# A plain second chunk instead of Strassen's, later rounding of weights, and keys of four pieces transposed by TensorE

## Chip, cores, metric

One core of one Trainium2 chip. The metric is the device time of one execution in microseconds, of the slowest core (there is one). The span in a profile is from the first to the last instruction and some 1 to 2 us shorter than the time. Lower is better.

## The reference, cut to what matters

```python
# attention: batch 8, heads 8, 576 positions, head_dim 64
scores = q @ k.T / 8
ret    = (scores * gamma_h ** (i - j) for j <= i, else 0) @ v      # no softmax
x = ret.transpose(0, 2, 1, 3).reshape(4608, 512)
# feed-forward: d_model 512, d_ff 2048
h = x @ w_in
g = h * erf(softplus(h))
out = g @ w_out                                                    # all in float32
```

## The kernel before

Tokens come in nine chunks of 512, each of four *pieces* of 128 (`PC = 4`); pieces 0 to 3 are chunk 0. A piece passes three stages: `transposes` (q and k with head_dim on partitions), `scores` (TensorE; VectorE masks the result into `sT`), and `outputs` (TensorE; VectorE scales the result into the chunk's `x`). These stages are laid between the matrix products of the feed-forward part, which runs in four groups (`g`) of hidden columns over the nine chunks: `First` is x times w_in, `Second` is g times w_out. The code calls a group's blocks of w_in `wa` and those of w_out `wb`; g is formed as t x s, with t for h and s for erf(softplus(h)). The attention stages share four buffers in PSUM, the memory that TensorE's results go to here; VectorE or ScalarE has to read a buffer before it is written again. In the first group all of this overlaps; in the other three, x is read back from HBM.

Both products use a Strassen form: seven block products in place of eight, at the price of sums on VectorE. Chunk 0 of the first group alone is `plain`, because its sums of weights are not ready:

```python
def plain(self):                       # 4 d-blocks x 4 accumulators x 2 = 32 matmuls
    for dc in range(n_dc):
        slots = (A12, A22) if dc // 2 else (A11, S3)      # S3 holds A21 until the sums are made
        for n in range(4):
            ...                                           # 2 matmuls, then yield

def operands_x(g, c):                  # Strassen: four sums of x on VectorE (three if g > 0)
    tt(t1, b12, b11, ALU.subtract)
    tt(t2, b22, t1, ALU.subtract)
    tt(b12, b22, b12, ALU.subtract)
    tt(t4, b21, t2, ALU.subtract)

def sums_in(a11, s3, a12, a22, s1, s2, s4):               # four sums of w_in's blocks
    ...
    tt(s3, a11, s3, ALU.subtract)      # from here on A21 is gone
```

Weights are rounded before use, in steps: ScalarE two passes, VectorE four (lines L252 to L265), then a product and an addition that GpSimd does for w_out (`wb`) and for all later groups. Keys and queries of pieces 0 to 7 come as rows and are transposed by TensorE and copied by ScalarE; from piece 8 on they come as *squares* of 32x32 and are transposed by VectorE:

```python
SQUARES = 2 * PC
...
if i >= SQUARES:
    nc.vector.transpose(out=tT..., in_=squares[:, :, :, :SQ])
else:
    nc.tensor.transpose(pt[:, p, :], flat(t[name][:, 2 * p : 2 * p + 2, :]), ident)   # 4 of them
    nc.scalar.copy(out=tT, in_=pt)
```

The order of the beginning is a string (`a` one attention stage, `p` one step of the plain chunk, `w` one load of weights, a digit so many rounding steps). The order matters because VectorE's work stands in the traces in the order in which the program emits it: in the prediction's timeline a rounding of w_out, 57.01 to 61.03 us, comes before the masked scores of 61.95 us that TensorE waits for.

## Time and profile before

| | before |
|---|---|
| time, median of 4 runs | 1034.19 us (1033.63 to 1035.70) |
| TensorE busy | 1017.5 of a span of 1035.3 us |
| VectorE busy, whole span | 65% |
| VectorE busy, 67 to 97 us | 29.5 of 29.8 us |
| start of piece 7's scores; of the second block's T2 product | 57.46; 97.08 us |

How to read it: the share over the span says that TensorE is the bound and VectorE is not. The line for 67 to 97 us says the opposite for that stretch. The prediction below shows these lines. One more line marks the end of the stretch, the first product of g's sums with w_out (T2); columns of this timeline are start, duration, engine, line, operation, operands:

```profile
97.08 1.99 PE L594 MATMUL a<-wb,s 128*128 128x256 f32 x8
```

The order of TensorE's instructions is the same in both kernels up to piece 7's outputs and from T2 on, so I measure both kernels between the start of piece 7's scores and T2: 97.08 - 57.46 = 39.62 us before.

### The profile page before, as it was taken

Reading aid. Unit: us, or ns where it says so; the run is one execution under the profiler, and the core shown is the slowest. Engines: PE = TensorE matmul, PEld = TensorE weight load, DVE = VectorE, ACT = ScalarE, POOL = GpSimd, SP = SyncE. Lnnn points to the kernel's source line nnn. Section 1 sums busy time; section 2 is a strip of 40 time slices with the busy share of each in tenths; the row PEclk is TensorE's granted clock in tenths of the full one; section 3 lists DMA queues with packets and bytes.
Section 4 is the critical chain, followed back from the end, with each engine's and each line's share of the span. In section 5 each row is a group of like instructions: output and inputs, shape, how many; then the busy total and the mean of one; then the engine's idle time right before and its main releaser. Section 6 shows DMA issues by size and latency. Waiting matters only on the chain.

```text
span 1035.3 us, 15922 instructions
## 1 busy us (share of the span) xinstructions
PE 1017.5 (98%) x6322; PEld 875.1 (85%) x6322; DVE 677.5 (65%) x1063; ACT 388.1 (37%) x477; POOL 124.3 (12%) x122
## 2 busy tenths in 40 slices
PE   8988999999999999999999999999999999999998
PEld 7767888887788888888888888888888888888887
DVE  3898778777777555667666656666666655555555
ACT  2353133242343544433434334444443333333332
POOL 2142112222312110100001000100100000000000
PEclk9989999999999999999999999999999999999999
DMA  9989979979983544444445444444433334444433
GB/s 192 202 200 223 248 150 251 216 179 245 216 211 124 204 142 142 143 142 144 169 161 161 155 147 142 145 159 167 143 122 122 123 122 131 132 130 133 127 88 117
DMA packets 148778, 167.27 MB, mean 162 GB/s; under 512 B 97632, under 2 KB 123360, under 8 KB 140640
## 3 DMA queue, kind: packets, MB, share of 16 engines
q1 hardware_dynamic: 147696, 165.47, 57.2%
q8 instruction: 50, 0.82, 0.4%
q10 hardware_dynamic: 1008, 0.79, 0.3%
q14 instruction: 24, 0.20, 0.1%
HBM read 119.02 MB, written 47.19 MB: 161 GB/s over the span
## 4 chain that ended last, share of the span: by engine, by line
PE 85%; DMA 7%; DVE 3%; SPq 3%; issue 1%; ACT 1%; POOL 0%; DVEq 0%; POOLq 0%
PE a L594 23%; PE a L486 22%; PE g L594 11%; PE g L486 11%; PE e L594 6%; PE e L486 5%; DMA raw_v<-in_v_dram 3%; PE s L339 2%; PE o L357 2%; DMA raw_qs<-in_q_dram 1%; DMA raw_ks<-in_k_dram 1%; SPq L130 1%; SPq L144 1%; PE o L380 1%; PE o L368 1%
## 5 line engine op out<-in xcount | busy, mean ns | idle before, releaser
L486 PE MATMUL a<-x,wa 128*128 128x256 f32 x1120 | 266.4, 381 | 0.0
L486 PEld LDWEIGHTS a<-x,wa 128*128 128x128 f32 x1120 | 211.8, 190 | 29.6
L594 PE MATMUL a<-wb,s 128*128 128x256 f32 x864 | 205.7, 381 | 0.0
L594 PEld LDWEIGHTS a<-wb,s 128*128 128x128 f32 x864 | 162.9, 190 | 23.6 <-ACT o L608 0.7
L99 DVE TENSOR_TENSOR t<-g,t 128x512 f32<-128x512 f32 x70 | 48.2, 689 | 150.9 <-ACT t L516 113.1
L486 PE MATMUL g<-x,wa 128*128 128x256 f32 x560 | 133.1, 380 | 0.0
L486 PEld LDWEIGHTS g<-x,wa 128*128 128x128 f32 x560 | 105.7, 190 | 14.9
L99 DVE TENSOR_TENSOR o<-a,o 128x512 f32<-128x512 f32 x108 | 74.1, 686 | 50.5 <-PE a L594 50.5
L511 ACT COPY t<-a 128x512 f32<-128x512 f32 x35 | 20.5, 586 | 189.6 <-PE a L486 189.6
L99 DVE TENSOR_TENSOR t<-t,s 128x1024 f32<-128x1024 f32 x72 | 88.8, 1274 | 0.0
L555 ACT ACTIVATE s<-t 128x1024 f32<-128x1024 f32 x72 | 72.1, 1049 | 32.0 <-DVE t L99 32.0
L267 POOL TENSOR_TENSOR wraw<-wraw 128x512 f32<-128x512 f32 x28 | 29.7, 1059 | 433.8 <-DVE wraw L265 176.6
L99 DVE TENSOR_TENSOR x<-x 128x512 f32<-128x512 f32 x116 | 77.8, 703 | 1.2
L522 ACT COPY t<-a 128x512 f32<-128x512 f32 x35 | 20.5, 586 | 151.9 <-PE a L486 151.9
L559 ACT ACTIVATE s<-s 128x1024 f32<-128x1024 f32 x72 | 72.1, 1048 | 0.4
L594 PE MATMUL a<-wb,t 128*128 128x256 f32 x288 | 68.6, 381 | 1.1 <-DVE t L99 1.1
L594 PE MATMUL e<-wb,t 128*128 128x256 f32 x288 | 68.6, 381 | 0.0
L594 PE MATMUL g<-wb,s 128*128 128x256 f32 x288 | 68.6, 381 | 0.0
L594 PE MATMUL g<-wb,t 128*128 128x256 f32 x288 | 68.2, 380 | 0.0
L486 PE MATMUL e<-x,wa 128*128 128x256 f32 x280 | 66.8, 381 | 0.0
L99 DVE TENSOR_TENSOR o<-g,o 128x512 f32<-128x512 f32 x72 | 49.3, 684 | 25.7 <-ACT o L608 20.9
L99 DVE TENSOR_TENSOR sT<-s,cst 128x512 f32<-128x512 f32 x72 | 46.1, 680 | 29.7 <-PE s L339 29.7
(75 smaller groups left out, 1202.6 us busy)
## 6 DMA issues: line engine op xcount, KB each, us to landing
od<-o SPq DMA_DIRECT2D x54, 512.0 KB, 3.4
x<-xd SPq DMA_DIRECT2D x27, 1024.0 KB, 4.8
o<-od SPq DMA_DIRECT2D x27, 1024.0 KB, 5.1
raw_qs<-in_q_dram SPq DMA_DIRECT2D x96, 112.0 KB, 4.6
raw_ks<-in_k_dram SPq DMA_DIRECT2D x96, 112.0 KB, 4.3
xd<-x SPq DMA_DIRECT2D x9, 1024.0 KB, 5.4
raw_k<-in_k_dram SPq DMA_DIRECT2D x64, 128.0 KB, 4.5
raw_v<-in_v_dram SPq DMA_DIRECT2D x64, 128.0 KB, 4.5
```

The lines of the kernel that those rows point to most:

```text
L99: nc.vector.tensor_tensor(out=out, in0=in0, in1=in1, op=op)
L130: nc.sync.dma_start(out=t[part * SQ : (part + 1) * SQ, :, at : at + m - SQ], in_=tokens[:, :, d0 : d0 + m - SQ])
L144: nc.sync.dma_start(out=t[r0 : r0 + n, e::2, :], in_=heads.rearrange("h p d -> p h d"))
L267: engine.tensor_tensor(out=r_f, in0=high_f, in1=r_f, op=ALU.mult)
L339: nc.tensor.matmul(ps[e][:, p, :], lhsT=t["kT"][heads[e], p, :], rhs=t["qT"][heads[e], p, :], start=True, stop=True)
L357: nc.tensor.matmul(o[p % 2][heads[(e + p) % 2], p // 2, :], lhsT=t["v"][:, 2 * p + e, :], rhs=t["sT"][:, e, p, :], start=(p < 2), stop=(no ...
L486: nc.tensor.matmul(acc[:, j * TH : (j + 1) * TH], lhsT=weights["wa", self.g][:, a, d, j * P : (j + 1) * P], rhs=x[self.g, self.c][a][:, d, :],
L511: nc.scalar.copy(out=self.t1[:, 1], in_=self.a)
L522: nc.scalar.copy(out=self.t2[:, 0], in_=self.a)
L555: nc.scalar.activation(self.s[:, j], t, AF.Softplus)
L559: nc.scalar.activation(self.s[:, j], self.s[:, j], AF.Erf)
L594: nc.tensor.matmul(acc[:, tp, :], lhsT=left[:, j * TH + tp * P : j * TH + (tp + 1) * P], rhs=weights["wb", self.g][:, b, j, :], start=(sta ...
```

## The change

The intent: give the early stretch, where VectorE is the bound, less VectorE work and a better order. Three parts: the second chunk `plain` too, so that its sums of x and additions are not needed and the sums of wa can wait; rounding of w_out moved behind the attention stages that TensorE waits for; keys of pieces 8 to 11 (`SQUARES_K`) as rows through TensorE.

```diff
+    SQUARES_K = 3 * PC
...
                     t["qs"] = load_squares(i, "q", q)
-                    t["ks"] = load_squares(i, "k", k)
-                elif name == "v" or len(pieces[i]) == 1:
+                    if i >= SQUARES_K:
+                        t["ks"] = load_squares(i, "k", k)
+                elif name == "v" or i < SQUARES_K or len(pieces[i]) == 1:
...
-                yield src, "wa", g, a, dc % 2, sums_in if dc == n_dc - 1 else None
+                yield src, "wa", g, a, dc % 2, ["wa"] if g > 0 and dc == n_dc - 1 else []
...
-                    yield src, "wb", ..., sums_out if (f, j) == (1, GP - 1) else None
+                    sums = (["wb"] if g > 0 else ["wb", "wa"]) if (f, j) == (1, GP - 1) else []
...
+    PLAIN = 2                                   # operands_x: chunks 0 and 1 unsummed in HBM
-        if g == 0 or c == 0:
+        if g == 0 or c < PLAIN:
...
-    for what in "alkakakawkakakawaa3awwa2aaa5ppappawwppa5ppapp5awwcpp4a5ppapp5aa5s1":
+    for what in "alkakakawkakakawaa3awwa2aaa5ppappawwppa5ppapp5wawcppa5ppappaa5s":
...
     firsts[0].softplus()
+    firsts[0].erf()
     most[0] = before_chunk(3)
-    attend(after_chunk(1) + 1)
-    operands_x(0, 1)
-    for step, _ in enumerate(firsts[1].first()):
-        attend(done[0] + 1)
-        round_weights((4, 2)[step])
-    firsts[0].erf()
-    firsts[0].multiply()
+    attend(after_chunk(1))
+    store_x(1)
+    for step, _ in enumerate(firsts[1].plain()):
+        if step % 2 == 0:
+            attend(min(done[0] + 1, most[0]))
+        round_weights(int(step > 1))
+        if step == 4:
+            firsts[0].multiply()
+        elif step == 8:
+            firsts[0].sums()
     seconds[0].begin()
+    run(seconds[0].first(), (2, 2))
+    firsts[1].softplus()
+    most[0] = before_chunk(4)
-    for b, nxt in zip(blocks[1:], blocks[2:] + [None]):
+    for b, nxt in zip(blocks[2:], blocks[3:] + [None]):
```

More of the change, by code (lines that the diff above doesn't have):

```diff
@@ L198, in parts @@
                     src = [(slice(0, P), w_out[ft * P : (ft + 1) * P, :].rearrange("p (h o) -> p h o", h=2))]
-                    yield src, "wb", g, B21 if f else B11, j, sums_out if (f, j) == (1, GP - 1) else None
+                    sums = (["wb"] if g > 0 else ["wb", "wa"]) if (f, j) == (1, GP - 1) else []
+                    yield src, "wb", g, B21 if f else B11, j, sums
     def sums_in(a11, s3, a12, a22, s1, s2, s4):
@@ L271, in rounding @@
             yield
-            if sums:
-                for step, _ in enumerate(sums(*(w[:, i] for i in range(7)))):
+            for n in sums:
+                of = (sums_in if n == "wa" else sums_out)(*(operands(n, g)[:, i] for i in range(7)))
+                for step, _ in enumerate(of):
                     if step == 3:
-                        rounded.add((name, g))
+                        rounded.add((n, g))
                     yield
@@ L312, in transposes @@
             tT = t[name + "T"] = att.tile([P, NP, P], FP32, tag=name + "T", name=name + "T")
-            if i >= SQUARES:
+            if name + "s" in t:
                 for _, _, n, r0 in pieces[i]:
```

## The prediction

> **What bounds the kernel now.** I read the page's first part, then the table of stretches, then TensorE's waits, then the timelines of TensorE and VectorE where the waits are.
>
> First part of the page (engine, busy us, share of the span, instructions):
>
> ```profile
> PE 1017.5 (98%) x6322; PEld 875.1 (85%) x6322; DVE 677.5 (65%) x1063; ACT 388.1 (37%) x477; POOL 124.3 (12%) x122
> ```
>
> TensorE is busy for 1017.5 of 1035.3 us. All that a change can win without taking work from TensorE is the 18 us in which it stands still, and time in which it runs at a lower clock. The change adds work to TensorE, so the question is whether it removes more standing still than it adds.
>
> The table of stretches, core 0, columns PE, PEld, DVE, ACT, POOL busy, granted clock, DMA share, GB/s:
>
> ```profile
> 45.94:57.46 11.52, 11.52 (x110) 9.58 (x108) 10.99 (x19) 6.78 (x12) 2.56 (x3) 1.00 0.65 167
> 57.46:67.28 9.82, 5.72 (x68) 4.49 (x64) 7.77 (x13) 2.62 (x5) 6.10 (x6) 0.69 0.78 201
> 67.28:97.08 29.80, 26.70 (x251) 21.30 (x249) 29.52 (x47) 10.78 (x13) 10.03 (x8) 0.99 1.18 246
> 97.08:123.04 25.96, 25.96 (x252) 21.17 (x249) 19.72 (x31) 8.01 (x10) 6.29 (x7) 1.00 0.91 226
> ```
>
> Between 57 and 67 us TensorE is busy only 5.7 of 9.8 us and is granted 0.69 of its clock. From 67 to 97 us VectorE is busy 29.5 of 29.8 us: there VectorE is the bound, and nowhere else for so long. From 97 us on TensorE runs without a hole. Of the rest of the 18 us, about 2.5 us lie at 240, 275 and 281 us, 4.2 us after the last matmul, some 2.6 us in the first 26 us; the change touches none of these.
>
> TensorE's waits from 45 to 97 us (line, waited for, us, times, longest):
>
> ```profile
> PE o L357 <- POOL wraw L267: 4.1, 1, 4.1
> PE a L594 <- DVE t L99: 1.1, 1, 1.1
> PE o L357 <- issue: 1.1, 1, 1.1
> PE p L540 <- DVE wa L268: 0.7, 1, 0.7
> PE s L339 <- DVE kT L318: 0.6, 1, 0.6
> ```
>
> The longest is booked on GpSimd, but a wait for several semaphores goes to the one that came last by the profile. The timelines of TensorE and VectorE show the real one:
>
> ```profile
> 57.46 1.16 PE L339 MATMUL s<-qT,kT 64*128 64x128 f32 x16
> 62.72 2.52 PE L357 MATMUL o<-sT,raw_v 128*64 128x128 f32 x16 [4.09 <-POOL wraw L267]
> ...
> 57.01 1.15 DVE L256 TENSOR_SCALAR wb<-wb 128x512 uint32<-128x512 uint32 x1
> 58.19 1.65 DVE L260 SCALAR_TENSOR_TENSOR wb<-wraw,wb 128x512 uint32<-128x512 uint32 x1
> 59.88 1.15 DVE L265 TENSOR_SCALAR wraw<-wb 128x512 uint32<-128x512 uint32 x1
> ...
> 61.95 1.27 DVE L99 TENSOR_TENSOR sT<-s,cst 128x512 f32<-128x512 f32 x2
> ```
>
> Piece 7's scores are done at 58.6 us; the masked scores sT that its outputs need come only at 61.95 us, behind two rounds of rounding weights and the scaling of piece 6 in VectorE's order. VectorE is late because the program gave it four sums of wa (2.62 us from 50.66) and two roundings of wb before them.
>
> **What the Trainium skill says.** "TensorE: Matmul & The Clock Gate", Part 1: after about one idle window of 3.4 us the array falls to half its clock, and needs about as long a busy time to get it back. The trace agrees: after the 4.09 us hole the granted clock is 0.50 from 62.70 to 67.30 and 1.00 again from 69.7. "SBUF — State Buffer", Who interferes with whom: VectorE and GpSimd share a port pair as a lock, held for a whole instruction. The trace agrees: the L260 form takes 0.69 us alone and 1.65 beside GpSimd's product at 57.95. "VectorE: DVE Perf Modes", The three transpose paths: VectorE transposes in 32x32 blocks into SBUF, TensorE a full 128x128 into PSUM, so a copy must follow. Here VectorE's key transpose of a piece has a median of 1.09 us; four TensorE transposes start 0.44 us apart as a group (pt_q 46.91, pt_k 47.35, next 47.79) and ScalarE's copy takes 0.59 us.
>
> **The change, part by part.** The order of instructions shows that TensorE's sequence is the same up to the outputs of piece 7 and the same again from the second block's T2 product on (at 97.08 us before). So the gain or loss is made between 46 and 97 us.
>
> (a) Plain second chunk on TensorE. Strassen's seven products have 28 matmuls; the plain form has 32. Each is two instructions, and eight of them take 1.73 us when nothing else comes between (spacing in the chain, 330 us and later). Four matmuls more: +1.7 us, all on the path, since TensorE is full.
>
> (b) Keys by TensorE. Four pieces by 0.44 us: +1.8 us on TensorE. ScalarE gets four copies, 2.3 us, with 37% busy: hidden. VectorE loses 0.73 + 3 x 1.06 = 3.9 us.
>
> (c) VectorE loses besides: four sums of x (3.9 us at 69.48, 2.6 in other chunks) and three additions of t (2.0 us). With the keys, 9.8 us of the 46 us that it works from 50.7 to 97 us. In each later group one more sum of x, 0.7 us, in stages where VectorE is about 60% busy: nothing.
>
> (d) The four sums of wa move from 50.66 us to after the roundings; a rounding of wb moves behind each piece. So the masked scores of piece 6 come at about 50.8 and not 53.2, the first rounding of wb ends at about 54.3, and VectorE stands idle when piece 7's scores end at 58.6. The first sT then comes 0.65 us later: the 4.1 us wait becomes 0.7 to 1: -3.2 us. The clock is not lost: 4.6 us of work at 0.50 take 2.3, and the next 2.4 us at 0.87 save 0.3: -2.6 us.
>
> (e) The waits at 78.9, 83.1 and 86.1 us (0.65 + 1.13 + 1.05 = 2.8 us; the last is from a busy VectorE too) should mostly go, since the keys, the products t x s and the x sums no longer stand in a row there. I leave 0.8 us: -2.0 us.
>
> (f) DMA: the squares of keys of four pieces are not loaded (about 4 x 4 x 112 KB), piece 8's rows are (256 KB): 1.5 MB less at 246 GB/s, 6 us of a DMA that is saturated from 67 to 97 us. It pays for the earlier start of everything behind; I book no gain.
>
> Sum: +1.7 + 1.8 - 3.2 - 2.6 - 2.0 = -4.3 us. A second way: writing the new order down with the measured durations, from the end of piece 7's scores to the T2 product. Outputs of piece 7 end at about 62.1 (67.28 before); the stretch to T2 was 29.8 us, of which 2.8 waits and 0.5 lost clock, so 26.5 of work, plus 3.5 gives 30.0: T2 at about 92.1 against 97.08, -5.0 with no wait left, and -4.2 with 0.8. I take -4.5: **1029.5 us**.
>
> **Rivals.** First: new waits eat the gain. Three places: the second sum of wb needs GpSimd's last rounding, and VectorE stands behind it ahead of piece 10's sT; x of piece 8 goes into the buffer of chunk 0, whose store must have landed (by my account 69.5 to 71 us, wanted at 72.3); ScalarE has softplus and erf, 6.6 us with both table loads, in front of piece 8's key copy. Against it: each has 1 us or more of room in my account, and VectorE has 9 us less to do. If one or two fail, 2 to 4 us come back: 1032 to 1034. Second: the added TensorE work is all that is left, because the wait at 62.72 comes anyway, from raw_v or data. The raw_v that it also needs is ready at 60.7 us before, itself behind GpSimd's rounding; with the first rounding earlier this moves to about 58. If the hole stayed, the time would be 1034 + 3.5 - 2 = 1035.5. Third: DMA relief goes on and also removes the waits at 240 to 281 us, or VectorE's slack keeps all of (e): 1026 to 1027. Those late waits are for key squares of later pieces behind stores in one queue, whose order is unchanged, so I think this is less likely than the first.
>
> **Range and chances.** Best case, every hole from 57 to 97 us and half of the late ones gone: about 1025. Worst plausible, the rival with the hole left or a new one with its loss of clock: 1035. Eight in ten: 1025.0 to 1034.0. 2% is 20.7 us, more than all of TensorE's standing still, so faster by over 2% has a chance of 0.01; slower by as much would need several new holes with lost clock: 0.01; within 2%: 0.98.
>
> **What would show it.** Right: TensorE's instructions 24 more and busy time about the same or a little less (the slow instructions gone); no clock of 0.50 between 57 and 70 us; the outputs of piece 7 ending near 62 us and T2 near 92.5; VectorE's busy time some 8 us less; after T2 the same spacing as before. Step (d) is wrong if a hole over 3 us stays before the outputs of piece 7; (e) if TensorE waits over 1.5 us between there and T2; (f) if new waits for input pieces come after 100 us. A wait that lasts past one idle window anywhere in the stretch would cost its length and some 2.5 us of clock, and make the prediction wrong.

## The result, and the profile after

The changed kernel took 1028.08 us (1027.37 to 1028.72, 4 runs) against 1034.19: ratio 0.9938, 95% interval 0.9921 to 0.9956. Taken again (e12 below) it took 1027.16 against 1035.65, ratio 0.9918 (0.9904 to 0.9931). Ratios are the mean time of one kernel's runs over that of the other's of the same rounds, so not quite the ratio of the medians quoted. The results are correct. The intervals together show a gain of 0.4 to 1.0%.

First part of the page, after; then the table of stretches, with the same columns as before:

```profile
PE 1017.5 (99%) x6346; PEld 876.1 (85%) x6346; DVE 669.1 (65%) x1054; ACT 390.4 (38%) x481; POOL 123.7 (12%) x122
```

```profile
45.94:57.46 11.52, 11.52 (x119) 9.66 (x119) 7.95 (x15) 7.35 (x13) 4.29 (x4) 1.00 0.88 211
57.46:62.00 4.54, 3.57 (x60) 2.73 (x57) 4.03 (x9) 4.50 (x5) 1.25 (x3) 1.00 0.70 159
62.00:92.00 30.00, 29.88 (x278) 24.48 (x277) 24.11 (x43) 11.87 (x18) 11.48 (x12) 1.00 1.06 251
```

TensorE has 24 instructions more (8 matmul, 16 transpose) and the same busy time: the added work stands where matmuls at half clock stood. From 62 to 92 us it is busy 29.88 of 30 us at full clock, and VectorE is no longer full (24.1 of 30). TensorE's waits of the whole run:

```profile
PE idle L706 <- POOL ident masks.py:199: 1.4, 1, 1.4
PE o L361 <- POOL state L423: 0.8, 1, 0.8
PE pt_k L328 <- DMA raw_k<-in_k_dram: 0.7, 2, 0.4
PE p L546 <- DVE wa L271: 0.7, 1, 0.7
PE s L343 <- DVE kT L322: 0.2, 1, 0.2
```

The 4.1 us are 0.8, and the three waits of 0.6 to 1.1 us between piece 7's outputs and T2 have gone. TensorE's timeline at the same place as in the prediction and at T2, then VectorE's:

```profile
56.78 1.16 PE L343 MATMUL s<-qT,kT 64*128 64x128 f32 x16
58.76 1.64 PE L361 MATMUL o<-sT,raw_v 128*64 128x128 f32 x16 [0.82 <-POOL state L423]
...
90.72 1.99 PE L600 MATMUL a<-wb,s 128*128 128x256 f32 x8
```

```profile
53.53 0.43 DVE L268 TENSOR_SCALAR wraw<-wb 128x512 uint32<-128x512 uint32 x1
56.30 0.42 DVE L99 TENSOR_TENSOR x<-o,cst 128x256 f32<-128x256 f32 x1 [2.34 <-PE o L372]
...
57.97 1.29 DVE L99 TENSOR_TENSOR sT<-s,cst 128x512 f32<-128x512 f32 x2 [0.25 <-PE s L343]
```

VectorE is done with its first rounding at 54 us, idles for piece 6's outputs, and idles again 0.25 us for piece 7's scores: now it waits for TensorE. From piece 7's scores to T2 it is 90.72 - 56.78 = 33.94 us, 5.68 us less than before.

The two profiled spans differ by 9.3 us, more than the medians (6.1). The profiled run of the kernel before was one of its long ones (1037.07 us). It is 0.7 us behind already at piece 7's scores, where the order of instructions is still the same, and from T2 to the end it takes 938.2 us against 935.3 after. In that last part it has 2.5 us of waits at 240 to 281 us that the changed kernel's two profiles hardly have (0.2 us and none). I do not count these as the change's doing: in the other kernels below these last waits vary from none to 3.2 us in sum. So the profiles place about 5.7 us of the gain in the stretch; what lies behind T2 is left open.

### The profile page after: what moved, and what is told of

The parts are those of the page before. It is cut to its first block, busy times and chain, and to the rows that moved or that the text cites.

```text
span 1026.0 us, 15946 instructions
## 1 busy us (share of the span) xinstructions
PE 1017.5 (99%) x6346; PEld 876.1 (85%) x6346; DVE 669.1 (65%) x1054; ACT 390.4 (38%) x481; POOL 123.7 (12%) x122
## 4 chain that ended last, share of the span: by engine, by line
PE 89%; DMA 5%; DVE 3%; SPq 3%; issue 1%; POOL 0%; DVEq 0%; POOLq 0%
PE a L600 23%; PE a L492 22%; PE g L600 11%; PE g L492 11%; PE e L600 6%; PE e L492 5%; PE s L343 3%; PE o L361 2%; DMA raw_qs<-in_q_dram 1%; PE p L546 1%; SPq L145 1%; PE o L384 1%; PE o L372 1%; DMA raw_k<-in_k_dram 1%; SPq L131 1%; DMA raw_ks<-in_k_dram 1%
## 5 line engine op out<-in xcount | busy, mean ns | idle before, releaser
L492 PE MATMUL a<-x,wa 128*128 128x256 f32 x1088 | 258.3, 380 | 0.0
L492 PEld LDWEIGHTS a<-x,wa 128*128 128x128 f32 x1088 | 205.7, 190 | 28.5
L492 PE MATMUL g<-x,wa 128*128 128x256 f32 x544 | 129.2, 380 | 0.0
L492 PEld LDWEIGHTS g<-x,wa 128*128 128x128 f32 x544 | 102.8, 190 | 14.4
```

The lines of the kernel that those rows point to most:

```text
L492: nc.tensor.matmul(acc[:, j * TH : (j + 1) * TH], lhsT=weights["wa", self.g][:, a, d, j * P : (j + 1) * P], rhs=x[self.g, self.c][a][:, d, :],
```

## The experiments

Twelve kernels, all runs fast and all results but e4's correct, in three calls of four kernels, each call on one chip with its own runs of the kernel before (medians 1034.93, 1034.65 and 1035.65). "Stretch" is from the start of piece 7's scores to T2 in the profile, "waits" are TensorE's in that stretch, from one profile of each kernel; the two profiles of the changed kernel differ by 0.3 us.

| kernel | plain | late roundings | keys by rows | time us | ratio to before | stretch us | waits us |
|---|---|---|---|---|---|---|---|
| before | no | no | none | 1034.19 | 1 | 39.6 | 6.9 |
| changed | yes | yes | 8-11 | 1028.08 | 0.9938 | 33.9 | 0.8 |
| e12, changed again | yes | yes | 8-11 | 1027.16 | 0.9918 | 33.6 | 0.8 |
| e1 | no | no | 8-11 | 1034.3 | 0.9991 | 39.1 | 6.3 |
| e9 | no | yes | none | 1035.45 | 0.9997 | 39.7 | 8.0 |
| e7 | no | yes, wa sums late | none | 1037.51 | 1.002 | 41.3 | 8.0 |
| e10 | no | yes | 8-11 | 1035.94 | 1.0003 | 41.8 | 8.5 |
| e2 | yes | yes | none | 1034.39 | 0.9991 | 41.8 | 7.0 |
| e11 | yes | yes | 8, 9 | 1029.9 | 0.9937 | 33.7 | 1.1 |
| e3 | yes | yes | 8-15 | 1030.07 | 0.995 | 33.6 | 0.8 |
| e8 | yes, store later | yes | none | 1034.58 | 0.9993 | 37.5 | 5.2 |
| e6 | yes | yes | 8-11, squares loaded too | 1036.35 | 1.0012 | 40.7 | 6.3 |
| e4 (wrong result) | yes | yes, wa sums early | 8-11 | 1029.14 | 0.9938 | 33.8 | 1.5 |
| e5 | yes | all but one of wb | 8-11 | 1029.63 | 0.9948 | 36.7 | 2.4 |

**e1: keys alone.** In the kernel before, only the `SQUARES_K` parts of the diff.

> The kernel before with the key transposes of pieces 8 to 11 on TensorE alone, Strassen's second chunk and the order of rounding as before. Theory (the gain is the hole of 4.1 us before the outputs of piece 7, with its half clock, and keys do not touch it): the hole stays, TensorE gets 1.8 us of transposes, VectorE loses 3.9 us in the stretch from 67 to 97 us where it is the bound, so of the 2.8 us of short waits there about 2 go: 1034 (1033 to 1035.5), no gain. Rival (VectorE's and DMA's relief by the keys carries the gain): 1029 to 1031.

1034.3 us, ratio 0.9991 (0.9978 to 1.0004): as the theory says. TensorE's waits in it:

```profile
PE o L359 <- POOL wraw L269: 4.1, 1, 4.1
PE pt_k L326 <- DVE x L99: 1.9, 1, 1.9
```

The hole stays. A new wait comes, for a PSUM buffer that VectorE has yet to empty, so the short waits are 2.2 us in place of 2.8: they do not shrink by the 2 us that I expected.

**e2: the change without keys.** `SQUARES_K = 2 * PC` in the changed kernel.

> The changed kernel with keys of pieces 8 to 11 as squares on VectorE again. Theory (after the hole is gone TensorE is the bound, and VectorE stands idle about 5.8 us between 62 and 90 us, in which 3.9 us of key transposes have room): TensorE loses 1.8 us, some 0 to 1 us of new waits: 1026.5 to 1027.5. Rival (the keys were moved because VectorE or DMA is short there): 1030 or more, with TensorE waiting for kT.

1034.39 us, ratio 0.9991 (0.9978 to 1.0004): my theory was wrong here and the rival right. TensorE's and then VectorE's timeline:

```profile
79.12 1.53 PE L361 MATMUL o<-sT,raw_v 128*64 128x128 f32 x15 [1.45 <-issue]
...
87.53 2.08 PE L343 MATMUL s<-qT,kT 64*128 64x128 f32 x16 [4.38 <-DVE kT L322]
```

```profile
67.46 1.29 DVE L99 TENSOR_TENSOR sT<-s,cst 128x512 f32<-128x512 f32 x2 [3.07 <-DMA cst<-in_decays_dram]
...
71.61 1.10 DVE L322 STREAM_TRANSPOSE kT<-raw_ks 128x512 f32<-128x512 f32 x1 [1.49 <-DMA raw_ks<-in_k_dram]
...
86.30 1.09 DVE L322 STREAM_TRANSPOSE kT<-raw_ks 128x512 f32<-128x512 f32 x1 [1.53 <-DMA raw_ks<-in_k_dram]
```

VectorE stands waiting for DMA, 6.1 us in these three lines: for the second part of the constants, and for the key squares of pieces 9 and 10. So it is not its amount of work alone that makes it late. The hole on TensorE before piece 7 is gone, and one of 4.4 us, again with half clock after it (piece 10's scores take 2.08 us for 1.16), stands before piece 10.

**e8: is it the store ahead of those loads?** e2, with the 1 MB store of chunk 1's x later:

```diff
     attend(after_chunk(1))
-    store_x(1)
...
         elif step == 8:
             firsts[0].sums()
+            store_x(1)
```

> e2 (keys as squares on VectorE) with the store of the second chunk's x (1 MB) issued after the loads of pieces 10 to 12 in the queue and not ahead of those of piece 10. In e2 piece 10's scores waited 4.4 us for key squares that landed at 86.3 us behind this store, and half the clock was lost after it. Theory (what the keys by rows bought is DMA time ahead of piece 10, not VectorE's time): the hole of 4.4 us and the 3 us of clock go, 1.5 us of another wait stays: 1027 (1026 to 1028.5). Rival (VectorE's 3.9 us of transposes themselves are what is too much): 1033 to 1035 as e2.

1034.58 us, ratio 0.9993 (0.9977 to 1.0008): the time that the rival gave, not my theory. The hole before piece 10 shrank from 4.38 to 2.67 us, without loss of clock, and the stretch from 41.8 to 37.5 us. VectorE's transpose of piece 10's keys no longer waits for DMA; the waits for the constants (2.8 us) and for piece 9's key squares (1.5 us) stayed and kept VectorE late. So this store was one cause in e2 and not the whole, and VectorE's amount of work is not excluded as another.

The 4.3 us are lost again behind T2, at least in the run that was profiled: from T2 to the end it takes 940.3 us against 936.5 in e2. It has 3.2 us of waits there (e2 has 1.3), and behind the last of them the clock is 0.50 from about 242 to 245 us, so that eight instructions take 3.67 us and not 1.99:

```profile
240.57 1.16 PE L343 MATMUL s<-qT,kT 64*128 64x128 f32 x16 [1.97 <-DVE kT L322]
241.66 3.67 PE L492 MATMUL g<-x,wa 128*128 128x256 f32 x8
```

That run was one of the longest of e8 (1036.32 us; they go from 1031.41 to 1036.37).

**e6: the loads without the work.** The changed kernel, key squares of pieces 8 to 11 loaded into tiles that nobody reads:

```diff
-                    if i >= SQUARES_K:
-                        t["ks"] = load_squares(i, "k", k)
+                    squares_k = load_squares(i, "k", k)
+                    if i >= SQUARES_K:
+                        t["ks"] = squares_k
```

> The changed kernel with the key squares of pieces 8 to 11 loaded too, into tiles that nobody reads: DMA as in e2 and 0.25 MB over it, engines as in the changed kernel. Theory (the DMA time ahead of pieces 9 and 10 is what counts): q squares and stores land later, new waits of 2 to 6 us on TensorE before 90 us, perhaps with clock lost: 1031 to 1036. Rival (VectorE's relief is the gain, DMA has room): 1028 to 1028.5.

1036.35 us, ratio 1.0012 (0.9999 to 1.0025), a little above the expected range: some 8 us lost by loads alone, with VectorE's and TensorE's work as in the changed kernel. The line of TensorE's timeline with the longest wait:

```profile
73.85 1.09 PE L329 MATMUL pt_k<-ident,raw_k 128*128 128x128 f32 x4 [5.49 <-DMA raw_k<-in_k_dram]
```

Piece 9's key rows are issued behind the unused squares of pieces 8 and 9 and land at 73.8 us; in the changed kernel this transpose ran at 67.98. SyncE, whose queue issues these loads, shows where the delay arises, in e6 (first fence) and in the changed kernel (second); the last line of each issues piece 9's key rows:

```profile
58.40 4.19 SPq L131 DMA_DIRECT2D raw_ks<-in_k_dram  x8
...
65.49 2.81 SPq L131 DMA_DIRECT2D raw_ks<-in_k_dram  x4
68.52 0.94 SPq L145 DMA_DIRECT2D raw_k<-in_k_dram  x2
```

```profile
62.77 0.98 SPq L145 DMA_DIRECT2D raw_k<-in_k_dram  x2
```

Issuing the twelve unused transfers takes SyncE 7.0 us. From the start of piece 7's scores, the key rows are issued after 11.2 us in e6 and after 6.0 us in the changed kernel, about the 5.5 us of the wait; from issue to landing the four loads of key rows at that place take a median of 5.2 us in both. So in e6 the rows come late because they are issued late, not because they move more slowly. Whether fewer bytes in as many transfers would help was not tried.

With e2 this shows what the keys by rows bought above all: an earlier place in the DMA queue for what pieces 8 to 10 need. VectorE's 3.9 us by themselves were not put back alone; in e2 VectorE waits for DMA longer than that, and e8 leaves open what they cost.

**e3: more keys.** `SQUARES_K = 4 * PC`.

> The changed kernel with keys of pieces 12 to 15 by TensorE as well. Theory (TensorE is full from 92 us, so its 4 x 0.44 us of transposes are paid in full and the relief of VectorE and DMA buys nothing more): 1029.9 (1029 to 1031). Rival (DMA relief still buys something): 1027 to 1028.

1030.07 us, ratio 0.995 (0.9938 to 0.9962). The profile has no wait of TensorE after T2, and T2 to end took 936.8 us against 935.0 in e12, which has none either: 1.8 us, the four times 0.44 us of transposes paid in full.

**e11: fewer keys.** `SQUARES_K = 2 * PC + 2`.

> The changed kernel with keys by rows for pieces 8 and 9 only, squares for 10 and 11. Theory (the DMA time ahead of piece 9's rows is what has to be free; one piece of squares later has room): TensorE saves 0.9 us and waits no more than 0.5: 1027 to 1027.7, at the limit of what the rounds resolve. Rival (any square load before 90 us comes late): 1029 to 1032.

1029.9 us (1026.94 to 1031.76), ratio 0.9937 (0.9920 to 0.9954): in the stretch as expected (33.7 us, TensorE waits 1.1), but the spread of the time is larger than the 0.9 us in question. The time lies in the rival's range and not in mine, but the intervals of e11 and e12 overlap: it neither beats the changed kernel nor is shown to be slower.

**e4: sums of wa early again.** In the changed kernel, the four sums behind wa's last rounding, as before (`pp4a5pp` in the string).

> The changed kernel with the four sums of wa (2.6 us) back in front of the first rounding of wb; nothing else. Theory (the hole came from the roundings of wb in front of piece 7's masked scores, and the sums only add to it): piece 6's masked scores come 2.6 us later, at about 54, still about when they are wanted, and VectorE's idle 2.3 us before piece 6's scaling takes up the rest: 1028 (1027.5 to 1029). Rival (the sums were what made VectorE late): the hole is 2 to 3 us again and the time 1030 to 1032.

1029.14 us, ratio 0.9938 (0.9925 to 0.9951), and a wrong result (relative error 0.157), which I had not foreseen: the sums overwrite A21, which a plain second chunk still reads. So they had to move, for the result. The time tells what it was for: piece 7's outputs wait 1.5 us in place of 0.8, the stretch is 33.8 us. With the roundings late, the early sums cost some 0.6 us of wait and no more.

**e5: the second rounding of wb early again.** In the changed kernel's string `a5ppappaa5s` becomes `a5ppapp5aas`.

> The changed kernel with the second rounding of wb back in front of piece 6's scaling, as before; the sums of wa stay late. Theory (a second rounding there, waiting for ScalarE and running beside GpSimd's products, makes piece 7's masked scores late): the wait before the outputs of piece 7 grows from 0.8 to 2 or 3 us, too short for half clock: 1029.5 to 1031. Rival (without the sums VectorE has room for both roundings): 1028.

1029.63 us, ratio 0.9948 (0.9937 to 0.996). The wait before piece 7's outputs is 2.4 us and the stretch 36.7 us, 2.8 more than in the changed kernel. TensorE's line, and VectorE's for the masked scores that it needs:

```profile
60.33 2.02 PE L361 MATMUL o<-sT,raw_v 128*64 128x128 f32 x16 [2.40 <-POOL wraw L270]
```

```profile
59.54 1.28 DVE L99 TENSOR_TENSOR sT<-s,cst 128x512 f32<-128x512 f32 x2
```

The profile books the wait on GpSimd, as before. But the first of the two masked scores is done at 60.23 us, 0.1 us before the outputs start; in the kernel before it is done at 62.62 and the outputs start at 62.72, in the changed kernel 58.66 and 58.76. So it is VectorE that they wait for. Of the 2.8 us more in the stretch about 1.2 are lost clock, which I had not expected from so short a wait. The table of stretches in steps of 1 us, where the granted clock is the last column but two:

```profile
59.00:60.00 1.00, 0.00 (x0) 0.00 (x0) 1.00 (x3) 0.98 (x2) 0.92 (x2) 1.00 0.78 312
...
61.00:62.00 1.00, 1.00 (x14) 0.95 (x14) 0.00 (x0) 0.99 (x2) 0.74 (x2) 0.72 1.07 252
62.00:63.00 1.00, 1.00 (x19) 0.72 (x16) 0.00 (x0) 1.00 (x2) 0.00 (x0) 0.50 1.19 210
```

A hole of 2.4 us was enough to lose half the clock for some 3 us, after it had ended. So one misplaced rounding is enough to make such a hole, and here it cost its length and clock besides. Up to these outputs VectorE's work differs from that in the kernel before in the sums of wa, which are absent here: with them the hole was 4.1 us.

**e7 and e9: late roundings with Strassen's second chunk.** e7, in the kernel before: `...ppapp5wawcppa5ppappaa5s`, sums of wa behind the second chunk's first product, `round_weights((9, 7)[step])`. e9: sums of wa early, `...ppapp5wawcpp4a5ppappaa5s` and `(5, 7)`.

> The kernel before with the new order of rounding alone: second rounding of wb behind piece 7's masked scores, third behind the outputs of piece 7, the sums of wa after the second chunk's first Strassen product, which they allow; Strassen's second chunk and key squares stay. Theory: the hole of 4.1 us before the outputs of piece 7 goes, but VectorE has 4.8 us more to do in a stretch that it fills already, and piece 10's key squares are as late as in e2; both give most of it back: 1031 to 1034. Rival (the order is the gain, the plain chunk and keys are not needed): 1025 to 1028.

> The order of the roundings alone, done better than in e7: as e10 but with keys as squares on VectorE. Theory (the hole of 4.1 us goes, but VectorE gets 2.2 us more behind it where it is full, and the key squares of pieces 9 and 10 come late): 1031 to 1035. Rival (the order is the gain): 1025 to 1028.

1037.51 us, ratio 1.002 (1.0008 to 1.0032), and 1035.45 us, ratio 0.9997 (0.9983 to 1.0011). In both the hole of 4.1 us is down to 0.8 and 1.4 us, and comes back where VectorE gets to the moved work: 3.1 us on a sum of wa and 3.7 us on the products t x s in e7, 5.5 us on t x s in e9. Both times are above what I expected. e7's excess is partly my placing of the sums.

**e10: the change without the plain chunk.** e9's order and `SQUARES_K = 3 * PC`.

> The change without its plain chunk: Strassen's second chunk stays (so the sums of wa stay early), the second and third roundings of wb go behind piece 7's masked scores and outputs as in the change, keys of pieces 8 to 11 by TensorE from rows. Theory (VectorE, which in the changed kernel is idle some 5.9 of 30 us from 62 to 92 us, has no room for the 5.9 us of sums of x and additions of t that Strassen needs, and stands them in front of piece 8's and 9's scores): TensorE's 1.7 us come off, 4 to 7 us of waits come: 1030 to 1034. Rival (order and keys are the gain, the plain chunk only costs): 1026 to 1027.

1035.94 us, ratio 1.0003 (0.9991 to 1.0015), again above the expected range. TensorE's timeline at its longest wait, then VectorE's ahead of it:

```profile
84.38 1.11 PE L326 MATMUL pt_k<-ident,raw_k 128*128 128x128 f32 x4 [7.11 <-DVE x L99]
```

```profile
64.66 4.48 DVE L99 TENSOR_TENSOR x<-x 128x512 f32<-128x512 f32 x4
...
79.36 1.51 DVE L99 TENSOR_TENSOR wb<-wb 128x512 f32<-128x512 f32 x1 [2.29 <-POOL wb L270]
80.80 3.20 DVE L99 TENSOR_TENSOR t<-t,s 128x1024 f32<-128x1024 f32 x2
83.91 0.74 DVE L99 TENSOR_TENSOR x<-o,cst 128x256 f32<-128x256 f32 x2
```

TensorE waits 7.1 us for a PSUM buffer that VectorE empties (x of piece 8 at 83.9 us) only behind the sums of x, the sums of wb and t x s. For 2.29 us of this VectorE itself stands idle, for GpSimd's last addition to wb, and it does so for 2.29 us in e7 and e9 as well: that part is my placing of wb's sums ahead of t x s and not VectorE's amount of work. A finer order of VectorE's work in a Strassen chunk could do better than mine; I did not try one, so these three runs do not show that the plain chunk is needed.

**e12: the changed kernel again.**

> The changed kernel as it is, on the same chip as the three above and with a second profile: 1028 (1027 to 1029); TensorE's waits after the second block's T2 product show whether the waits at 240 to 280 us of the kernel before are a matter of the run.

1027.16 us, stretch 33.6 us, no waits after T2. No kernel beats it.

## Why the prediction was right

1029.5 us was predicted, 1028.08 measured, inside the range. The gain was 6.1 us where 4.7 were predicted; by the ratios it is 6.4 and 8.5 us. Most of its signs were seen: 24 instructions more on TensorE, no clock of 0.50 in the stretch, the outputs of piece 7 ending at 61.5 us, 8.4 us less work on VectorE. T2 came at 90.7 us, earlier than the 92.5 forecast. By its steps:

- **(a), (b), TensorE's added work, 3.5 us: right.** The four key transposes took 0.44 to 0.46 us each in the timeline, and e3 shows the same 1.8 us for four more. Added up from the timelines, the sixteen plain steps take 15.2 us and the seven Strassen products before 13.2, without waits and lost clock: 2.0, predicted 1.7.
- **(d), the hole, -3.2 us, and its clock, -2.6: right.** 4.09 us became 0.82, -3.27. Outputs of piece 7 and the product after them took 2.3 us less. The reading that VectorE's order and not GpSimd was behind it is borne out by e5, where one rounding put back makes 2.4 us of it again, and by the end of the masked scores 0.1 us before the outputs start. The sums of wa were the smaller part: without them but with the second rounding early the hole is 2.4 us and not 4.1 (e5), with the roundings late they cost 0.6 us (e4). One reading of the prediction was incomplete: it gives the half clock from 62.70 us, after the hole; stretches of 0.5 us show 0.60 from 61.0 and 0.50 from 61.5 us, so it began within the hole.
- **(e), the short waits, -2.0: too small.** 2.83 us went, all of it, and pieces 8 and 9's outputs and the first products with w_out ran another 1.1 us closer. These are the differences between -4.3 and the measured -5.68 of the stretch: -3.27 - 2.28 - 2.83 + 3.74 - 1.06 is -5.70.
- **(f), DMA, no gain booked: right as a sum, and its weight missed.** I wrote that it "pays for the earlier start". e6 puts this payment at some 8 us (piece 8's key rows are loaded there too), and e2 shows that without it the other two parts gain nothing (the loads' order in the queue differs too, e8). I reckoned it in bytes; what delayed the rows in e6 was the time that SyncE needs to issue. The first rival named three places for new waits, and none of them was piece 9's or 10's keys. Its first place, the sum of wb behind GpSimd, does show where Strassen's chunk stays: 2.29 us on VectorE in e7, e9 and e10.
- **The sum of parts as a way of reckoning was luckier than it looks.** Each part or pair that I ran without the rest, five of them, gives a ratio between 0.999 and 1.002: keys (e1), roundings (e7, e9), roundings and keys (e10), plain chunk with roundings (e2). The plain chunk alone and with keys without late roundings I did not run as such; e5, with one of the roundings early, is 1 to 3 us worse by the ratios. In these runs three things took turns at being late in this stretch (VectorE's order, what stands ahead of t x s on VectorE, DMA), and the time came only when all three were out of the way. That the plain chunk is the only way to clear the second is argued and not shown.

Open: the waits of 0 to 3.2 us at 219 to 281 us, which vary between kernels and profiles; what VectorE's key transposes cost by themselves; a better order with Strassen's chunk kept.

## What to carry to other kernels

When several parts of a change clear one stretch, take them out singly before believing a sum: here the five kernels that had only some of the parts gained nothing, since the next late engine or queue took over the hole. Giving a nearly full TensorE 3.7 us more work paid because it kept VectorE and the DMA queue clear, so that the hole which the new order removes did not come back a few us later; beyond that point the transposes added in e3 were paid in full. A load that is off the path in the kernel before can be what a faster stretch waits for, so ask of each transfer where it stands in the queue once everything before it comes 5 us earlier.

## What the Trainium skill lacked or had wrong

- "TensorE: Matmul & The Clock Gate", Part 1, gives about one idle window of 3.4 us for falling to half clock. As a safe limit for a hole that is too long here: holes of 2.40 us in e5 (0.50 from about 61.5 to 64.5 us, beginning after the hole's end) and of 1.97 us in e8 (at 240 us) were enough. Length alone does not decide: a hole of 2.67 us in e8 cost no clock, one of 3.09 us in e7 did.
- The same page calls the window free-running, and the traces fit that: the clock changes at 6.82, 61.43 and 64.84 us in e5 and at 6.29, 241.81 and 245.23 us in e8, whole multiples of 3.41 us apart. But in the window that ends at e5's fall TensorE stands still for 2.3 of 3.4 us only, so an idle window is not one without any work. What share counts as idle is open: the hole of 2.67 us in e8 lies across two such windows with 2.0 and 0.7 us.
- The same page's start-to-start times are for bf16 and have no figure for float32 operands. Here each 128x128 by 128x256 float32 matmul is two instructions, eight take 1.73 us, so 0.43 us a matmul; a float32 transpose of 128x128 is one instruction, four in 0.44 us.
- "VectorE: DVE Perf Modes", The three transpose paths, compares the paths by their own time. What decided here was the layout that each path asks of the load: the squares of a piece's keys are 4 x 112 KB more in DMA where rows are loaded anyway. Loading four pieces of them unused cost some 8 us, and issuing the first twelve of these transfers took SyncE 7.0 us (e6).
